# A first phase in another written order, with another share of VectorE's and GpSimd's work, and block 1's first product in another PSUM bank

## The chip, the cores and the metric

The kernel runs on one core of a Trainium2 chip. The metric is the time of one execution on the device, in microseconds (us). Before the change the median of three runs was 705.74 us (705.36 to 707.13).

The engines, as the profile names them: PE is TensorE (matmuls), PEld its weight loads, DVE is VectorE, ACT is ScalarE, POOL is GpSimd, SP is SyncE, which here only issues transfers. Each engine works through its own queue in the order in which the program was written.

## The reference

For each of 8 batches (8 heads, 576 rows, head width 64), 32 packed queries first attend over the rows, and the rows then attend over the 32 packed results. Then a gated feed-forward step with 2048 hidden columns runs on all 4608 rows.

```
s = q @ k.T / sqrt(64); s = s - max(s); a = exp(s); a = a / (sum(a) + 1e-9)   # sm_attn(q, k, v) = a @ v
p_packed = sm_attn(p, k, v)
out      = sm_attn(q, p_packed, p_packed)          # per batch and head
x = out, heads side by side: (4608, 512)
h = x @ w_in                                       # (4608, 2048)
g = h * clip(h + 3, 0, 6) / 6
result = g @ w_out                                 # (4608, 512)
```

The two weights come in as 64-bit floats; everything else is 32-bit.

## The kernel before

The hidden columns are cut into 16 blocks of 128, numbered f = 0 to 15. For a batch the kernel does not form x: it multiplies the packed results with `w_in` once (the matrix m), so that h is a product of the row weights a and m. Every factor of a large product is kept as two parts, `hi` (rounded) and `lo` (the rest), and a product is three matmuls: hi by hi, lo by hi, hi by lo.

The first batch runs in a first phase of its own, with the making of the weights and the attention of the second batch woven in; the other seven batches follow in a steady loop that the change does not touch. The order of the first phase stands in a table, `PLAN`: some 600 words, each the name of a chain. A chain is a generator (a list of steps); at each word the next step of that chain is written, and its instruction goes to the end of its engine's queue. So the table sets the order in all queues at once, SP's too. A second table, `ENGINES`, says on which engine a step runs where there is a choice (`on` and `copy`, lines 309 to 316).

The chains that matter here:

- `liF`, `loF` load block F of `w_in` and `w_out`; `in` was one chain for all inputs of the first batch, in a fixed order.
- `aF` (`w_in_step`) makes block F of `w_in` in 32 bits: two passes on ScalarE (L255, L257), a shift on VectorE (L261), an addition on GpSimd (L265). `bF` (`w_out_step`) does the same for `w_out`, then copies the hi part (L275) and subtracts for the lo part (L277).
- `m0`, `m1`, `m2`, `m4`, `m8`, `m12` (`u_m0`) multiply the packed results with blocks 0, 1, 2 to 3, 4 to 7, 8 to 11 and 12 to 15 of `w_in` (L336), and split the result (L347, L349). `m4` needs the additions of blocks 4 to 7, `m8` those of 8 to 11.
- `z0`, `z1` are the scores of rows against packed results; `z0a`, `z1a`, `z1b` turn them into a: maximum (L923), subtraction (L925), exponential, sum, division (L935), transposition (L937), hi (L939) and lo (L941).
- `hF` (`first`, L670) is the first product of block F, `rF` (`gates`) its gate: relu on ScalarE (L1333), minimum and product on VectorE (L1335), hi part `gh` (L1340), lo part `gl` (L1342). `yF` copies the gate's edge columns (L1349). `xF` is the second product (L1037), twelve matmuls into four accumulators.
- `S`, `E`, `V`, `T`, `Z`, `M` are parts of the second batch's attention.

All first products `hF` write the same PSUM tile pair `ps_h0`, of which there is one: `h1` has to wait until the gate of block 0 has read it. Where PE would have nothing to do, `keep_busy` (L202) multiplies zeros: in `warm` (1, 2 and 3 times), before `m1`, in `z1`, in `v1` and, six times, before `m2`. A matmul in 32 bits leaves two records in the trace.

Of the kernel before, what the change touches and what calls it, by code (L numbers as in the profile page):

```python
# [94 lines left out]
s0 warm q1 e0 q1 c0 c0 q0 e0 li0 b2 in v0 q0 e1 c1 v0 in v0 s1 s1 a0 qr c1 qr v0 z0 a0 z0 a0 z0a li2 z0a z0a e1
z0a in v1 a2 a2 a2 in v1 z0a z0a q2 li1 q3 q3 q2 z0a z0a z0a v1 a0 v1 z1 z1 a1 a2 m0 a1 a1 z0a z1b z0a a1 m0 z1a
li3 z1b a3 a3 upper z1a m0 z1b z1b a3 z1a lo0 m0 z1b z1a m0 m1 warm b0 z0a li4 z1a a4 a4 z1a lo1 z1b a3 b0 b0
z1b z1a m2 b1 z1b z1a z1b z1b b0 z1a z1a li7 z1a b1 z1b a7 a7 lp b1 h0 a7 h0 r0 b1 r0 li5 m1 m1 warm m1 h1 b0 m1
# [10 lines left out]
Z x11 lo13 b13 b13 b13 y10 r12 r12 r12 b13 Z b13 Z Z x11 r12 h13 h13 x12 x12 x12 r13 y12 r13 Z b13 lo14 h14 b15
Z y12 b15 r13 Z b14 b14 r13 b14 h14 Z b14 x13 r14 r14 x13 Z b14 x12 Z y13 b14 h15 Z x13 r14 h15 r15 x13 r14 x14  # L110
Z Z x14 y15 M r15 r15 Z y13 r15 x15 x15 x14 Z Z x14 o0 Z o0 x15 Z x15 Z Z o1 stage M M y15 y14 M M o2 o2 o3 o3
o1 y14
# [22 lines left out]
def packed_attention_moe(  # L135
# [542 lines left out]
    def first_attention(chains, homes):  # L678
# [33 lines left out]
        def inputs():  # L712

            t = wr.tile([P, 2, 2 * NB], F32, name="k_nat0", tag="w_in1")
            nat["k", 0] = long_rows(k, 0, 4, t[:, 0])
            yield
            nat["p"] = ap.tile([P, NG, D], F32, name="p_nat0", tag="pn", bufs=1)
            nc.scalar.dma_start(out=nat["p"], in_=p[0].rearrange("(g h) i d -> (h i) g d", g=NG))
            yield
            nat["k", 1] = long_rows(k, 4, 4, t[:, 1])  # L720
            yield
            nat["kr"] = rest_rows(nc.scalar, room(15, H * 2 * D), k)
            yield
            for g in range(NG):
# [820 lines left out]
```

## Time and profile before

| | us |
|---|---|
| median of three runs | 705.74 (705.36 to 707.13) |
| span of the profiled execution | 702.6 |
| first phase, to the first matmul of the steady loop | 116.74 |
| PE busy | 690.6 (98%) |
| DVE busy | 500.5 (71%) |
| ACT busy | 428.7 (61%) |
| POOL busy | 386.8 (55%) |

The page has the profiled execution's time only as its span, from the first to the last instruction; the 3.1 us to the runs' median lie around it. A row of the timeline gives the start in us from the span's start, the duration, the engine, the source line, the operation, what it writes and reads, the partitions and elements, and in brackets the idle time before it with what ended it. The duration of a VectorE record that stood blocked holds the time it was blocked.

### The profile page before, as it was taken

What the parts mean: (1) busy time and instruction counts of PE and PEld (TensorE: products, weight loads), DVE (VectorE), ACT (ScalarE), POOL (GpSimd) and SP (SyncE); (2) the same over time, 40 slices, a digit from 0 to 9 for tenths busy, and PEclk for the clock granted to TensorE, in tenths of its full rate; (3) what the DMA queues carried; (4) which work ended last, traced back from release to release, by engine and by line L of the source; (5) the groups of instructions that cost most, each with busy time, mean ns of one, the idle gap of its engine ahead of it and who ended that gap; (6) DMA issues with size and microseconds to landing.
All of it is one profiled execution on the core that took longest, in us unless ns stands there. A gap on an engine that the chain in (4) does not pass through costs nothing.

```text
span 702.6 us, 16232 instructions
## 1 busy us (share of the span) xinstructions
PE 690.6 (98%) x5944; PEld 595.8 (85%) x5944; DVE 500.5 (71%) x1087; ACT 428.7 (61%) x1014; POOL 386.8 (55%) x620
## 2 busy tenths in 40 slices
PE   7899999999999999999999999999999999999997
PEld 5587877888979888898898988899898988989997
DVE  4898788768899669774687667876488766864443
ACT  4898886556656656564465655666366665755453
POOL 1556662545645565575554555566455646657563
PEclk9999999999999999999999999999999999999999
DMA  9989852983429665655446755483543835341030
GB/s 270 318 208 259 227 130 83 285 176 120 100 105 242 139 168 186 158 147 126 126 150 158 157 134 181 130 211 70 129 166 128 198 85 182 120 140 41 32 105 31
DMA packets 199104, 107.50 MB, mean 153 GB/s; under 512 B 173424, under 2 KB 185200, under 8 KB 195440
## 3 DMA queue, kind: packets, MB, share of 16 engines
q1 hardware_dynamic: 198480, 106.26, 55.4%
q8 instruction: 47, 0.77, 0.5%
q14 instruction: 33, 0.27, 0.1%
q10 hardware_dynamic: 544, 0.20, 0.1%
HBM read 89.65 MB, written 16.78 MB: 151 GB/s over the span
## 4 chain that ended last, share of the span: by engine, by line
PE 87%; DVE 6%; DMA 2%; ACT 2%; issue 1%; POOL 1%; SPq 0%; DVEq 0%; ACTq 0%
PE acc L1037 49%; PE ps_hh L997 24%; PE ps L413 6%; PE ps_h L670 3%; PE ps L1037 2%; PE ps L533 1%; DMA v_nat<-in_v_dram 1%; DMA room<-in_q_dram 1%; PE ps L503 1%; ACT t L1333 0%; DVE osb L1236 0%; SPq L706 0%; DVE t L1335 0%; PE ps L336 0%; DVE t L1009 0%
## 5 line engine op out<-in xcount | busy, mean ns | idle before, releaser
L997 PE MATMUL ps_hh<-a_hi,m_hi 128*128 128x320 f32 (+1 forms) x448 | 133.8, 299 | 0.4 <-PE acc L1037 0.3
L997 PE MATMUL ps_hh<-a_lo,m_hi 128*128 128x320 f32 (+1 forms) x448 | 132.9, 297 | 0.0
L997 PE MATMUL ps_hh<-a_hi,m_lo 128*128 128x320 f32 (+1 forms) x448 | 132.8, 296 | 0.0
L1009 DVE SCALAR_TENSOR_TENSOR t<-t,ps_hh 128x320 f32<-128x320 f32 (+1 forms) x148 | 66.0, 446 | 78.3 <-ACT t L1008 73.4
L1037 PE MATMUL acc<-wo_hi,g 128*128 128x512 f32 x288 | 103.4, 401 | 0.0
L1008 ACT ACTIVATE t<-ps_hh,three 128x320 f32<-128x320 f32 (+1 forms) x148 | 73.7, 500 | 44.8 <-PE ps_hh L997 39.3
L1015 POOL TENSOR_TENSOR gf<-tb,gf 128x256 fp32r<-128x256 f32 x76 | 62.3, 821 | 64.6 <-ACT gf L1014 57.9
L997 PEld LDWEIGHTS ps_hh<-a_hi,m_hi 128*128 128x128 f32 x448 | 84.7, 189 | 9.2 <-DVE t L1009 2.8
L997 PEld LDWEIGHTS ps_hh<-a_lo,m_hi 128*128 128x128 f32 x448 | 84.7, 189 | 4.4 <-issue 1.4
L997 PEld LDWEIGHTS ps_hh<-a_hi,m_lo 128*128 128x128 f32 x448 | 84.7, 189 | 2.2 <-issue 1.7
L1015 POOL TENSOR_TENSOR g<-t,g 128x256 fp32r<-128x256 f32 x72 | 55.1, 768 | 39.1 <-ACT g L1014 36.3
L1037 PE MATMUL acc<-wt,ga 128*128 128x256 f32 x456 | 74.4, 283 | 0.0
L1037 PE MATMUL acc<-wo_hi,ge 128*128 128x256 f32 x304 | 71.5, 285 | 0.0
L1037 PEld LDWEIGHTS acc<-wo_hi,g 128*128 128x128 f32 x288 | 52.8, 189 | 13.5 <-ACT g L1014 2.1
L1037 PEld LDWEIGHTS acc<-wt,ga 128*128 128x128 f32 x456 | 63.4, 190 | 0.7 <-issue 0.5
L1015 POOL TENSOR_TENSOR ga<-t,ga 128x256 fp32r<-128x256 f32 x76 | 60.5, 795 | 2.0 <-ACT ga L1014 1.8
L1037 PEld LDWEIGHTS acc<-wo_hi,ge 128*128 128x128 f32 x304 | 53.1, 190 | 6.6 <-issue 2.3
L1037 PE MATMUL acc<-wo_lo,g 128*128 128x512 f32 x144 | 56.8, 395 | 0.0
L618 DVE STREAM_TRANSPOSE tr<-nat 128x576 f32<-128x576 f32 x56 | 42.6, 767 | 18.2 <-DMA nat<-in_q_dram 8.8
L1008 ACT ACTIVATE tb<-ps_hh,three 128x256 f32<-128x256 f32 (+1 forms) x76 | 37.9, 499 | 26.5 <-PE ps_hh L997 24.9
L1279 POOL TENSOR_TENSOR tb<-tb,t 128x128 f32<-128x128 f32 x76 | 38.5, 507 | 27.4 <-DVE t L1274 26.7
L1033 POOL COPY bnd<-t 128x64 f32<-128x64 f32 x76 | 21.6, 284 | 55.1 <-DVE t L1009 54.9
(227 smaller groups left out, 1845.9 us busy)
## 6 DMA issues: line engine op xcount, KB each, us to landing
w_again<-w_kept SPq DMA_DIRECT2D x24, 1024.0 KB, 4.8
wt<-t_kept SPq DMA_DIRECT2D x24, 768.0 KB, 5.1
out_dram<-osb SPq DMA_DIRECT2D x33, 256.0 KB, 2.4
nat<-in_k_dram SPq DMA_DIRECT2D x112, 72.0 KB, 3.1
nat<-in_q_dram SPq DMA_DIRECT2D x112, 72.0 KB, 3.0
raw_in<-in_moe_w_in_dram SPq DMA_DIRECT2D x10, 512.0 KB, 6.1
raw_out<-in_moe_w_out_dram SPq DMA_DIRECT2D x10, 512.0 KB, 4.1
w_kept<-w_in_sb SPq DMA_DIRECT2D x4, 1024.0 KB, 7.5
```

What stands on the lines that cost most here:

```text
L413: nc.tensor.matmul(pair[x][NPK * a:NPK * a + NPK, :n], rows[half, a], c, start=True, stop=True)
L503: nc.tensor.transpose(out=pair[x][:, c * P:(c + 1) * P], in_=e[x][:, c * P:(c + 1) * P], identity=ident)
L533: nc.tensor.matmul(pair[x][cols, :D], l, r, start=(c == 0), stop=(c == NST - 1))
L618: nc.vector.transpose(out=t, in_=state.pop(("nat", which, b, a)))
L670: nc.tensor.matmul(h[:, hf, :HS], mm[:, g, fs], aa[:, hf * HS:(hf + 1) * HS], start=(g == 0 and i == 0), stop=(g == NG - 1 and i == 2),)
L997: state["first"] = nc.tensor.matmul(h[:, :n], mm[:, g, fs], aa[:, t0:t0 + n], start=(g == 0 and i == 0), stop=(g == NG - 1 and i == 2),)
L1008: state["relu"] = nc.scalar.activation(out=t[:, :n], in_=h, func=AF.Relu, bias=three)
L1009: state["gate"] = nc.vector.scalar_tensor_tensor(out=t[:, :n], in0=t[:, :n], scalar=6.0, in1=h, op0=ALU.min, op1=ALU.mult)
L1015: engine.tensor_sub(out=lo, in0=x, in1=hi.bitcast(F32))
L1033: nc.gpsimd.tensor_copy(out=bnd[:, f, side * REM:side * REM + REM], in_=t[:, boff:boff + REM])
L1037: nc.tensor.matmul(out, lhs[x], rhs[y], start=first and i == 0, stop=last and i == 2, skip_group_check=True)
L1279: nc.gpsimd.tensor_sub(out=s4, in0=b1, in1=s2)
```

## The change

The order table is new up to the second batch's transpositions (`E`); from there on the words are the same. The chain `in` is cut into eleven chains that stand apart in the table (`ik0`, `ip`, ...), so that rows 512 to 575 of the queries and their second quarter are loaded ahead of the values, and block 0 of `w_out` is loaded ahead of blocks 1 and 3 of `w_in`. More steps have a choice of engine (the hi copies `whF`, `ghF`, `mhF`, `ah`, and the subtraction `zs`), and the table `ENGINES` gives some steps to another engine. `h1` writes the pair of banks in which the first scores stood (`homes["w"]`); the word `upper`, where that pair is given away, stands later for it, and `m2` takes its banks from the accumulators that are not in use yet. The six matmuls by zero before `m2` are gone, and one `warm`.

```diff
 PLAN = """
-in k0 in in p p k0 k1 k1 k2 k2 lo2 in kr b2 b2 b2 b2 kr k3 k3 in in in b2 s0 s0 s0 s0 s0 s0 s1 s1 s1 s1 s1 s1 s0
+ik0 k0 ip ik1 p p k0 k1 k1 k2 k2 lo2 ikr iqr iq1 kr b2 b2 b2 b2 s0 kr k3 k3 iv0 s0 s0 b2 s1 s0 iq0 s0 s0 q1 s1 s1
...
 ENGINES = {
-    "gl2": "D", "wl3": "D", "wl4": "D", "bl3": "P", "gl3": "D", "wl5": "D", "bl4": "D", "gl4": "D",
+    "D", "bl3": "P", "gl3": "P", "wl5": "P", "bl4": "D", "gl4": "D", "bl2": "D", "gl5": "D", "bl5":
...
     def w_out_step(f):
         yield from narrowed(f, "out")
         x = state.pop(("w", "out", f))
-        nc.scalar.copy(out=wo_at("hi", f), in_=x)
+        copy(f"wh{f}", wo_at("hi", f), x)
...
         for x, ps in enumerate(banks):
-            nc.scalar.copy(out=hi[:, x, to], in_=ps[:, :n * P])
+            copy(f"mh{fs[0]}{x}", hi[:, x, to], ps[:, :n * P])
...
+            for i in range(2):
+                chains[f"ik{i}"] = keys(i)
+                chains[f"iv{i}"] = values(i)
+            for a in range(NPAIR):
+                chains[f"iq{a}"] = queries(a)
+            chains["ip"], chains["ikr"], chains["iqr"] = packs(), key_rest(), query_rest()
...
-            nc.vector.tensor_sub(out=z[:, w], in0=z[:, w], in1=across(mx))
+            on(f"zs{g}{w.start}", "D").tensor_sub(out=z[:, w], in0=z[:, w], in1=across(mx))
...
-            nc.scalar.copy(out=hi[:, cols], in_=at[:, cols])
+            copy(f"ah{g}{w.start}", hi[:, cols], at[:, cols])
...
         def first(f):
-            h = tops[f] = ps_h0.tile([P, 2, 512], F32, name="ps_h0", tag="w")
+            h = tops[f] = (homes["w"] if f == 1 else ps_h0).tile([P, 2, 512], F32, name="ps_h0", tag="w")
...
-            nc.scalar.copy(out=hi, in_=top)
+            copy(f"gh{f}", hi, top)
...
             if f in (2, 4, 8, 12):
-                chains[f"m{f}"] = u_m0(list(range(f, 4 * (f // 4 + 1))), ahead=6 * (f == 2))
+                chains[f"m{f}"] = u_m0(list(range(f, 4 * (f // 4 + 1))), homes["tail"] if f == 2 else None)
```

What the tables move is seen in the queues. First GpSimd's, from the addition of block 1 of `w_in` to that of block 6 (x_out is a block of `w_out`, w_in_sb a block of `w_in`). Before:

```order
L265 TENSOR_TENSOR w_in_sb_322<-w_in_sb_322,raw_in 128x512
L941 TENSOR_TENSOR a_lo<-room,a_hi 128x576
L265 TENSOR_TENSOR w_in_sb_322<-w_in_sb_322,raw_429 128x512
L935 TENSOR_TENSOR z<-z,den_396 128x288
L265 TENSOR_TENSOR x_out<-x_out,raw_out 128x512 x2
L265 TENSOR_TENSOR w_in_sb_525<-w_in_sb_525,raw_in 128x512
L265 TENSOR_TENSOR x_out<-x_out,raw_429 128x512
L265 TENSOR_TENSOR w_in_sb_525<-w_in_sb_525,room 128x512
L265 TENSOR_TENSOR w_in_sb_525<-w_in_sb_525,raw_612 128x512
L265 TENSOR_TENSOR w_in_sb_525<-w_in_sb_525,room 128x512
```

And now, the same stretch of GpSimd's queue in the changed kernel:

```order
L270 TENSOR_TENSOR w_in_sb_325<-w_in_sb_325,raw_in 128x512
L946 TENSOR_TENSOR z<-z,mx_399 128x288
L962 TENSOR_TENSOR a_lo<-room,a_hi 128x576
L270 TENSOR_TENSOR w_in_sb_325<-w_in_sb_325,raw_415 128x512
L956 TENSOR_TENSOR z<-z,den_400 128x288
L270 TENSOR_TENSOR x_out<-x_out,raw_out 128x512
L962 TENSOR_TENSOR a_lo<-room,a_hi 128x288
L270 TENSOR_TENSOR x_out<-x_out,raw_out 128x512
L1363 TENSOR_TENSOR gl<-t,gh 128x512
L270 TENSOR_TENSOR w_in_sb_514<-w_in_sb_514,raw_in 128x512
L1370 COPY bnd<-t 128x2x32
L270 TENSOR_TENSOR x_out<-x_out,raw_415 128x512
```

GpSimd has taken over from VectorE the subtraction of half of `z1` (L946), half of the lo part of a (the second L962) and the lo part of block 0's gate (L1363).

Then TensorE's queue at the seam of block 0's and block 1's first product (ps_h is the pair of banks they write; L202 and L207 are the matmuls by zero). Before:

```order
L670 MATMUL ps_h_518<-a_hi,m_hi 128x288
L670 MATMUL ps_h_518<-a_lo,m_hi 128x288
L670 MATMUL ps_h_518<-a_hi,m_lo 128x288
L202 MATMUL ps_t<-pps 128x256 x3
L670 MATMUL ps_h_545<-a_hi,m_hi 128x288
L670 MATMUL ps_h_545<-a_lo,m_hi 128x288
```

And now:

```order
L675 MATMUL ps_h_471<-a_hi,m_hi 128x288
L675 MATMUL ps_h_471<-a_lo,m_hi 128x288
L675 MATMUL ps_h_471<-a_hi,m_lo 128x288
L675 MATMUL ps_h_537<-a_hi,m_hi 128x288
L675 MATMUL ps_h_537<-a_lo,m_hi 128x288
L675 MATMUL ps_h_537<-a_hi,m_lo 128x288
```

The matmuls by zero between the two blocks are gone, and block 1's tile (537) lies in another bank pair than block 0's (471).

Last SP's queue of transfers behind the last query loads (raw_in is block 1 of `w_in`, raw_429 and raw_415 block 3, raw_out block 0 of `w_out`). Before:

```order
L706 DMA room<-in_q_dram 128x2x256 x2
L238 DMA raw_in<-in_moe_w_in_dram 128x4x256
L238 DMA raw_429<-in_moe_w_in_dram 128x4x256
L238 DMA raw_out<-in_moe_w_out_dram 128x1024
L238 DMA room<-in_moe_w_in_dram 128x4x256
```

And now:

```order
L713 DMA room<-in_q_dram 128x2x256 x2
L243 DMA raw_out<-in_moe_w_out_dram 128x1024
L243 DMA raw_in<-in_moe_w_in_dram 128x4x256
L243 DMA raw_415<-in_moe_w_in_dram 128x4x256
L243 DMA room<-in_moe_w_in_dram 128x4x256
```

Block 1 of `w_in` is now second behind the queries, and block 3 third.

## Rows read from the trace of the kernel before

**Rows 1.** The page's top: span, and busy time of each engine

```profile
span 702.6 us, 16232 instructions
PE 690.6 (98%) x5944; PEld 595.8 (85%) x5944; DVE 500.5 (71%) x1087; ACT 428.7 (61%) x1014; POOL 386.8 (55%) x620
```

**Rows 2.** Busy by stretch: length, PE, PEld, DVE, ACT, POOL, clock, DMA, GB/s

```profile
24.50:46.04 21.54, 19.53 (x129) 15.82 (x130) 19.31 (x45) 19.63 (x40) 14.44 (x11) 1.00 0.91 244
46.04:65.65 19.61, 19.33 (x139) 14.89 (x138) 16.39 (x31) 17.07 (x32) 11.43 (x12) 1.00 0.95 244
65.65:91.90 26.25, 26.25 (x253) 20.82 (x252) 20.17 (x41) 22.78 (x42) 16.98 (x17) 1.00 0.91 241
```

**Rows 3.** TensorE's timeline, 33 to 67 us

```profile
33.55 1.46 PE L202 MATMUL ps_t<-pps 128*128 128x256 f32 x6
35.49 0.37 PE L670 MATMUL ps_h<-a_hi,m_hi 128*128 128x288 f32 x1 [0.48 <-ACT wo_hi L275]
...
37.15 0.40 PE L1037 MATMUL acc<-wo_hi,gh 128*128 128x512 f32 x1
...
46.63 1.09 PE L336 MATMUL ps<-w_in_sb,pp 64*32 64x512 f32 x16
...
53.26 0.72 PE L413 MATMUL ps_w<-tr,p_tr 64*32 64x288 f32 x16 [0.28 <-DVE t L1335]
...
66.48 1.09 PE L336 MATMUL ps<-w_in_sb,pp 64*32 64x512 f32 x16
```

**Rows 4.** VectorE's timeline, 35 to 44 us

```profile
35.66 1.13 DVE L277 TENSOR_TENSOR wo_lo<-x_out,wo_hi 128x512 fp32r<-128x512 f32 x1
36.71 0.68 DVE L1342 TENSOR_TENSOR gl<-t,gh 128x512 fp32r<-128x512 f32 x1
37.31 0.68 DVE L277 TENSOR_TENSOR wo_lo<-x_out,wo_hi 128x512 fp32r<-128x512 f32 x1
37.92 0.41 DVE L261 TENSOR_SCALAR x_out<-raw 128x512 int32<-128x512 int32 x1
38.25 0.74 DVE L1335 SCALAR_TENSOR_TENSOR t<-t,ps_h 128x576 f32<-128x576 f32 x1
...
43.22 0.94 DVE L261 TENSOR_SCALAR w_in_sb<-room 128x512 int32<-128x512 int32 x1
```

**Rows 5.** GpSimd's timeline, 24 to 85 us

```profile
24.50 1.29 POOL L265 TENSOR_TENSOR w_in_sb<-w_in_sb,raw_in 128x512 int32<-128x512 int32 x1 [2.10 <-ACT raw_in L257]
...
30.17 0.81 POOL L935 TENSOR_TENSOR z<-z,den 128x288 f32<-128x288 f32 x1 [0.77 <-DMA room<-in_moe_w_in_dram]
...
34.94 1.29 POOL L265 TENSOR_TENSOR w_in_sb<-w_in_sb,raw_in 128x512 int32<-128x512 int32 x1
...
42.55 1.32 POOL L265 TENSOR_TENSOR w_in_sb<-w_in_sb,raw 128x512 int32<-128x512 int32 x1
...
64.33 1.32 POOL L265 TENSOR_TENSOR w_in_sb<-w_in_sb,raw_in 128x512 int32<-128x512 int32 x1 [1.11 <-ACT raw_in L257]
...
83.16 1.30 POOL L1342 TENSOR_TENSOR gl<-t,gh 128x512 fp32r<-128x512 f32 x1 [0.24 <-ACT gh L1340]
```

**Rows 6.** Busy and count in 24.50 to 65.65: L265, L261, L277, L1342

```profile
24.50:65.65 41.15, 23.25 (x17) 1.00 0.93 244
24.50:65.65 41.15, 8.00 (x16) 1.00 0.93 244
24.50:65.65 41.15, 4.98 (x6) 0.00 (x0) 1.00 0.93 244
24.50:65.65 41.15, 4.16 (x6) 0.00 (x0) 1.00 0.93 244
```

**Rows 7.** SP's timeline: issue of the load of block 3 of `w_in`

```profile
14.12 2.54 SPq L238 DMA_DIRECT2D raw<-in_moe_w_in_dram  x1
```

**Rows 8.** Transfers issued at 14.12: count, KB each, us to landing

```profile
raw<-in_moe_w_in_dram SPq DMA_DIRECT2D x1, 512.0 KB, 9.7
```

**Rows 9.** ScalarE's timeline: first pass over block 1 of `w_in`

```profile
23.15 0.71 ACT L255 ACTIVATE raw_in<-raw_in 128x512 f32<-128x512 f32 x1
```

More of the change, by code (lines that the diff above doesn't have):

```diff
@@ L93 @@
 PLAN = """
-in k0 in in p p k0 k1 k1 k2 k2 lo2 in kr b2 b2 b2 b2 kr k3 k3 in in in b2 s0 s0 s0 s0 s0 s0 s1 s1 s1 s1 s1 s1 s0
[L95 to L98, printed above, removed]
@@ L109 @@
[L109 to L112, printed above, removed]
+ik0 k0 ip ik1 p p k0 k1 k1 k2 k2 lo2 ikr iqr iq1 kr b2 b2 b2 b2 s0 kr k3 k3 iv0 s0 s0 b2 s1 s0 iq0 s0 s0 q1 s1 s1
+li0 warm s1 s0 e0 q1 c0 c0 q0 s1 s1 s0 e0 v0 v0 q0 c1 qr v0 iv1 e1 v0 li2 iq2 z0 s1 iq3 qr s1 z0 a0 a0 c1 e1 a0
@@ new lines @@
+z0a z0a lo0 z0a v1 a2 a2 z0a z0a a2 q2 li1 v1 q3 q3 v1 q2 b2 a1 z0a a0 z0a z0a v1 z0a a1 z1 z1 a2 z0a a1 z0a li3
+m0 z1a m0 z1b a3 z1a z1b z1a a3 a1 warm z1a z1b z1b m0 li4 m1 a3 z1b lo1 m1 z1a z1b z0a b0 z1a m0 z1a a3 b0 h0
+li5 m2 a4 b1 b0 z1a z1b z1b b0 b1 m0 z1b a4 z1a z1a m2 z1b z1a m1 li7 m2 m1 m1 a7 a7 a7 lp a4 z1b lo3 lo5 h0 li6
+r0 b1 h1 b0 r0 m2 h1 h2 b0 b1 m2 r0 r0 h2 r1 b1 x0 r1 x0 x0 b3 r1 a7 b3 b1 b3 y0 r1 b5 y0 y1 x1 x1 x0 y1 upper a6
+lo4 lo6 r2 h3 a5 b3 r2 x1 a5 a5 lk0 b4 a6 x1 a4 tk0 r2 a6 b4 r2 b4 b3 a5 x2 b5 y2 h3 lk2 a6 r3 b4 m4 x2 tk2 b3 x2
@@ new lines @@
+tp lk3 b5 r3 m4 r3 m4 h4 m4 li8 y3 tk3 b4 m4 lk1 h4 r3 x3 b6 b4 x3 tk1 b6 b6 r4 below y3 li9 a8 b5 a8 lo8 x2 S b6
+y4 b5 r4 y4 S S b5 a9 a8 li10 x3 S a8 S a9 x3 h5 r4 h5 a10 r4 x4 y2 b6 lq1 r5 x4 a9 r5 a9 b6 y5 a10 r5 S S b8 x4
+a10 a10 h6 r5 li11 b8 S x4 h6 b8 x5 r6 a11 a11 x5 x5 b8 b8 y5 S r6 x5 a11 a11 h7 h7 b8 m8 lo9 tq1 lq3 b9 S r6 r6
+lo7 b7 lo10 x6 b7 x6 li13 b7 tq3 lq2 x6 r7 y7 r7 b9 x6 m8 r7 m8 b7 m8 li12 h8 b10 m8 lq0 b7 h8 y7 b7 r7 x7 x7 b10
+y6 y6 x7 a13 r8 lo12 b10 r8 a13 b9 tq2 r8 b10 S S b10 lv r8 h9 h9 y8 r9 S S b10 x8 a13 x8 r9 tq0 a12 x7 y9 x8 h10
@@ new lines @@
+h10 a12 b9 S b9 E r9 S b12 E b12 r10 y10 E y8 lw1 y9 x8 r9 E a13 b9 x9 x9 S h11 a12 r10 a12 E E b12 r10 r10 lo11
+b11 h11 E b11 b11 r11 x10 r11 lw0 b11 li14 a14 V a14 V V a14 li15 x10 T b12 x9 T x9 a14 Z a15 a15 x10 a15 x10 Z Z
+r11 Z y11 lo15 Z b11 a15 b12 b15 m12 r11 b15 b11 m12 b15 b15 y11 x11 m12 m12 m12 b12 x11 h12 h12 Z x11 lo13 b13
+b13 b13 y10 r12 r12 r12 b13 Z b13 Z Z x11 r12 h13 h13 x12 x12 x12 r13 y12 r13 Z b13 lo14 h14 b15 Z y12 b15 r13 Z
+b14 b14 r13 b14 h14 Z b14 x13 r14 r14 x13 Z b14 x12 Z y13 b14 h15 Z x13 r14 h15 r15 x13 r14 x14 Z Z x14 y15 M r15
@@ L113 @@
+r15 Z y13 r15 x15 x15 x14 Z Z x14 o0 Z o0 x15 Z x15 Z Z o1 stage M M y15 y14 M M o2 o2 o3 o3 o1 y14
 """
 ENGINES = {
[10 rows of a table removed]
[16 rows of a table added]
 }
@@ L689, in tail @@
             return ps_o.tile([P, 512], F32, name="ps_t", tag=f"acc{(tails[0] - 1) % 4}", bufs=1)
+        homes["tail"] = tail
         def wide(i):
@@ L712, in inputs, with keys, packs, key_rest @@
         def inputs():
[L714 to L724, printed above, removed]
+            kt_ = wr.tile([P, 2, 2 * NB], F32, name="k_nat0", tag="w_in1")
+            def keys(i):
+                nat["k", i] = long_rows(k, 4 * i, 4, kt_[:, i])
+                yield
+            def packs():
+                nat["p"] = ap.tile([P, NG, D], F32, name="p_nat0", tag="pn", bufs=1)
+                nc.scalar.dma_start(out=nat["p"], in_=p[0].rearrange("(g h) i d -> (h i) g d", g=NG))
+                yield
+            def key_rest():
+                nat["kr"] = rest_rows(nc.scalar, room(15, H * 2 * D), k)
+                yield
+            def values(g):
                 t = wp.tile([P, 4 * NST * D], F32, name="v_nat0", tag="v_nat", bufs=1) if g == 0 else room(12, 4 * NST * D)
@@ L728, in inputs, with queries, query_rest @@
                 yield
-                for a in (2 * g, 2 * g + 1):
-                    nat["q", a] = long_rows(q, 2 * a, 2, room(4 + a, 8 * D))
-                    yield
-                if g == 0:
-                    nat["qr"] = rest_rows(nc.sync, room(10, H * 2 * D), q)
-                    yield
+            def queries(a):
+                nat["q", a] = long_rows(q, 2 * a, 2, room(4 + a, 8 * D))
+                yield
+            def query_rest():
+                nat["qr"] = rest_rows(nc.sync, room(10, H * 2 * D), q)
+                yield
+            for i in range(2):
[4 more added lines that the diff above has]
+            chains["ip"], chains["ikr"], chains["iqr"] = packs(), key_rest(), query_rest()
         def turn_rows(x, i, place):
@@ L955, in warm @@
                 yield
-        chains["in"] = inputs()
+        inputs()
         chains["warm"] = warm()
```

10 lines of the change are left out of this document (removed), and 24 rows, old and new, of the table ENGINES.

## The prediction

> **What bounds the kernel now.** I read the page's top first: PE is busy 98% of the span, and no other engine more than 71% [rows 1]. That says the steady loop runs at PE's pace, and the change does not touch that loop. So I read the first phase alone, by stretches. From 24.50 to 65.65 us PE is busy nearly throughout, but VectorE is at 90% and 84% of the two stretches, ScalarE at 91% and 87%, and GpSimd at 67% and 58% [rows 2]. A busy share of 67% looks like room. The next view, the timelines of VectorE and GpSimd side by side, shows that it is not.
>
> A lo part on VectorE (L277) and a lo part of the gate (L1342) take 0.68 us alone. The L277 at 35.66 took 1.13: GpSimd was in an addition from 34.94 to 36.23, and VectorE's operation ended at 36.79, so it began at about 36.11 (36.79 less 0.68). The shift L261 takes 0.41 alone; the one at 43.22 took 0.94, and GpSimd's addition beside it ran from 42.55 to 43.87 [rows 4, 5]. So these VectorE operations and GpSimd's do not run side by side: they take turns. I call the two together the pair: all that GpSimd does, the shift L261, and VectorE's operations on two tensors of SBUF. L277 is one of these; that L1342, L925, L935 and L941 take turns too I assume from their being of the same kind.
>
> How full is the pair? From the addition of block 1 of `w_in` (24.50) to that of block 11 (64.33, over at 65.65) are 41.15 us. In them stand 17 additions on GpSimd, 16 shifts, and 6 and 6 lo parts on VectorE [rows 6], and besides one a_lo of 576 columns, one division and three small copies on GpSimd, and five operations of 288 columns on VectorE. I price them by what one keeps the pair: an addition 1.29, the division 0.81 [rows 5]; a shift 0.33 (37.92 to 38.25) and a lo part 0.60 (36.71 to 37.31) [rows 4]. By columns, as estimates from these: a_lo 1.45 (1.29 x 576/512), a VectorE operation of 288 columns 0.34. The small copies are on both sides and are taken at 0.25, an estimate from the 1.29 for 512 columns. The sum is 17 x 1.29 + 1.45 + 0.81 + 0.75 + 16 x 0.33 + 12 x 0.60 + 5 x 0.34 = 39.1. Only 2.05 of 41.15 us are free. To this comes what overlaps when one engine hands over: above, VectorE began 0.12 before GpSimd's record ended. With about 20 such turns that is up to 2.4 more. Free in all: 2 to 4.4 us.
>
> PE meanwhile runs `m4` at 46.63 and `m8` at 66.48 [rows 3], 0.83 after the last addition that `m8` needs. So PE and the pair are both full, and whichever the change makes longer sets the end.
>
> **The change, part by part.** *Block 1's banks and the matmuls by zero.* Before, the six records of zeros at 33.55 and a wait of 0.48 fill the time until `h1` starts at 35.49 [rows 3]: 1.94 us, in which the gate of block 0 frees the banks. In other banks `h1` follows block 0's last matmul at once, so PE gains 1.94 there. The zeros ahead of `m2` also go; they stood in the wait for the second half of `z1`, which stays, so I cost them at nothing.
>
> Here the clock may answer. The granted clock is 1.00 in every stretch of [rows 2], with those zeros in place. [...] It is the third rival.
>
> *The loads.* Block 1 of `w_in` now stands second behind the queries; that place belonged to block 3, which was issued at 14.12 and landed 9.7 later, at 23.8 [rows 7, 8]. Everything ahead of it in the queue is the same set of loads in another order, so I take 23.8 as its landing. Before, ScalarE began on block 1 at 23.15 and GpSimd added at 24.50 [rows 5, 9], 1.35 later. Now ScalarE begins at about 23.8 and GpSimd at about 25.05 to 25.15, some 0.55 later. If the queries' new place brings the loads forward, the bound is zero.
>
> *The tables of engines.* To the addition of block 11 GpSimd gets four lo parts more (`gl0`, `gl3`, `wl5`, `wl6`) and two half operations (a subtraction of `z1`, half of a_lo). On GpSimd a lo part takes 1.30 (L1342 at 83.16) and a half operation 0.81 [rows 5]: 4 x 1.30 + 2 x 0.81 = 6.8. VectorE gives up 4 x 0.60 + 2 x 0.34 = 3.1. It gets two copies from SBUF to SBUF (`gh4`, `wh6`), of which this trace has no row: between the shift's 0.33, the same columns with one input, and the lo part's 0.60; I take 0.33, nearest by kind, so 0.7. [...] The stem of the matter: an operation moved off VectorE leaves 0.60 behind and asks 1.30 of the pair. The pair gets 6.8 - 3.1 + 0.7 = 4.4 us longer. VectorE itself gets 2.4 us shorter; that would count if VectorE alone, not the pair, set the pace.
>
> *What is late next.* GpSimd's queue is strict: the additions of blocks 8 to 11 stand behind the new lo parts. Before, the last ended at 65.65. Now it ends at 65.65 + 0.55 + 4.4 less what of the free 2 to 4.4 us gets filled: 70.6 at most, 66.2 at least. The queues are full and one engine mostly waits for the other, so part of the free time will be used: I take half of the 4.4, giving 68.4. PE, which gains 1.94 at `h1`, would reach `m8` at 64.5, waits at `m4` and `m8`, and starts `m8` at about 68.4 instead of 66.48: 1.9 us late. Behind `m8` PE is busy 26.25 of 26.25 us [rows 2] with the same work, so it cannot catch up, and the phase ends 1.9 later.
>
> **Sum.** Against the profiled span of 702.6 [rows 1]: 702.6 + 1.9 = 704.5. The runs' median of 705.74 is 3.1 above the span; I take that as unchanged: 707.6. With the pair's bounds, -0.2 to +4.1, this case alone lies between 705.5 and 709.8. A measurement of this kernel can tell about 0.3%, 2.1 us, from no change: faster is under 703.6, slower over 707.9. So the forecast itself lies just inside "no change", and its upper part outside.
>
> **The rivals.** *PE sets the pace (faster).* For it: PE is busy 19.53 of 21.54 and 19.33 of 19.61 us, VectorE loses 2.4 us of work, and the order could place the pair's turns without a gap. Then the 1.94 at `h1` stays, and with it the 0.28 wait at 53.26 [rows 3] goes: 705.74 - 2.2 = 703.5. Against it: the pair's sum, which would need more than all its free time.
>
> *The gain is given back (no change).* PE comes 1.9 earlier to `m4`, waits there, and the pair fills all of its 4.4 free us, so that `m8` starts where it did. 705.7. For it: the free time is just as long as what is added. Against it: the later start of block 1, and that no queue is without a gap.
>
> [...]
>
> **How the numbers follow.** Forecast 0.50, PE's pace 0.20, given back 0.17, clock 0.13. Slower by over 0.3%: the clock's 0.12 and about half of the forecast, 0.24, in all 0.36. Faster: 0.16 of PE's pace and a little beside it, 0.17. The rest, 0.47, is within 0.3%. The range takes in the first two rivals nearly whole and the upper bound of the pair: 703.5 to 710.0.
>
> **What would show it.** Right: `m4` and `m8` begin behind a wait for GpSimd (L270, additions of `w_in`), `m8` at 67.5 or later; GpSimd's and VectorE's records stretch each other more than before; `h1` follows block 0 without a gap; block 1's addition starts after 24.8. Wrong: `m8` before 66 with no wait ahead of it; block 1's addition before 24.5; or a stretch with a granted clock under 1.00, which would make the third rival the cause. If the steady loop, from its first matmul on, is not as long as before, something lies outside of all this.

## The result and the profile after

The changed kernel takes 710.76 us (median of 6, 709.84 to 712.08) against 706.36 for the kernel before on the same chip: a ratio of 1.006, with a 95% interval of 1.0042 to 1.0078, so 3.0 to 5.5 us longer. A second set gave 710.77 and 1.0064 (1.0043 to 1.0085). Two executions of one experiment below (the kernel before with cut additions), which took 950.77 and 1111.33 us at a granted clock of 0.66 and 0.56, are left out of its numbers. The forecast was 707.6, with 710.0 as the upper end: too low, and the likeliest case, "no change", did not come.

The top of the page of the changed kernel, to be held against [rows 1]:

```profile
span 709.9 us, 16191 instructions
PE 693.3 (98%) x5926; PEld 595.6 (84%) x5926; DVE 505.8 (71%) x1089; ACT 425.4 (60%) x1005; POOL 398.0 (56%) x627
```

The span grew by 7.3 us, the median by only 4.4. Both spans are single executions; a profiled execution's own time is its span and 1.8 (709.9 and 711.72 here). By that the profile of before was of a quick execution, some 704.4, and not of the median: of the 3.1 us that were said to lie around its span, only 1.8 do. For this reason I reckon from here on from `m0`, the first use of the finished weights: in a second profile of the kernel before (an experiment below) `m4`, `m8` and `m12` come within 0.05 us of where they came in the first, reckoned from `m0`.

The stretches `m0` to `m4`, to `m8`, to `m12`, first of the kernel before, then of the changed kernel (columns as in [rows 2]):

```profile
23.83:46.63 22.80, 20.79 (x172) 16.46 (x156) 20.50 (x47) 20.81 (x43) 14.45 (x11) 1.00 0.90 241
46.63:66.48 19.85, 19.57 (x142) 15.37 (x141) 16.47 (x31) 17.31 (x33) 12.25 (x12) 1.00 0.98 256
66.48:92.08 25.60, 25.60 (x248) 20.15 (x247) 19.68 (x41) 22.13 (x40) 16.15 (x15) 1.00 0.90 235
```

```profile
23.32:48.41 25.09, 20.32 (x154) 16.16 (x138) 22.28 (x44) 20.53 (x40) 18.20 (x15) 0.80 0.77 216
48.41:70.58 22.17, 20.56 (x143) 15.29 (x142) 20.24 (x31) 16.19 (x30) 15.60 (x13) 1.00 0.85 217
70.58:99.70 29.12, 26.65 (x246) 19.93 (x246) 22.73 (x47) 21.18 (x38) 17.85 (x15) 1.00 0.84 218
```

Each stretch is longer: by 2.29, 2.32 and 3.52 us. In all three VectorE and GpSimd are busier, and in the first the granted clock is 0.80 on average. From the first matmul of the steady loop (124.11) to the end the time is as before, 585.8.

The clock by pieces of 2 us:

```profile
28.00:30.00 2.00, 0.93 (x5) 0.70 (x5) 1.97 (x5) 2.00 (x4) 1.66 (x2) 0.86 1.11 320
30.00:32.00 2.00, 0.58 (x16) 0.26 (x16) 1.97 (x6) 0.79 (x2) 1.92 (x2) 0.50 1.03 371
...
36.00:38.00 2.00, 2.00 (x10) 2.00 (x10) 1.55 (x3) 1.81 (x4) 1.25 (x2) 0.50 0.92 146
38.00:40.00 2.00, 2.00 (x12) 2.00 (x11) 0.82 (x3) 1.45 (x3) 2.00 (x2) 0.58 0.48 69
```

TensorE had been busy 0.93 and then 0.58 of 2 us when the granted clock went to 0.50. TensorE's timeline, to be held against [rows 3]:

```profile
31.42 1.11 PE L341 MATMUL ps_t<-w_in_sb,pp 64*32 64x256 f32 x16 [2.04 <-DVE m_lo L354]
...
34.07 0.61 PE L675 MATMUL ps_h<-a_lo,m_hi 128*128 128x288 f32 x1 [0.92 <-DVE a_lo L962]
...
35.43 0.44 PE L675 MATMUL ps_h<-a_hi,m_hi 128*128 128x288 f32 x1
...
40.52 0.40 PE L1058 MATMUL acc<-wo_hi,gh 128*128 128x512 f32 x1
...
48.41 1.09 PE L341 MATMUL ps<-w_in_sb,pp 64*32 64x512 f32 x16
51.99 0.37 PE L675 MATMUL ps_h<-a_hi,m_hi 128*128 128x288 f32 x1 [0.90 <-DVE t L1356]
...
70.58 1.09 PE L341 MATMUL ps<-w_in_sb,pp 64*32 64x512 f32 x16 [0.28 <-POOL w_in_sb L270]
...
91.90 0.32 PE L538 MATMUL ps<-v_high,et 128*32 128x64 f32 x8 [1.17 <-DMA v_high<-in_v_dram]
...
99.70 1.09 PE L341 MATMUL ps<-w_in_sb,pp 64*32 64x512 f32 x16 [0.52 <-POOL w_in_sb L270]
```

`h1` does follow `h0` without a gap (35.43), but at a granted clock of 0.50 its matmuls start 0.24 apart instead of 0.13. `m2` waits 2.04 for its banks, which `m_lo` of `m1` reads. `x0` starts 17.20 after `m0` instead of 13.32; 1.6 of that is `h2`, which now stands ahead of it. The other 2.3 are all of the 2.29 by which `m4` is late: from `x0` to `m4` TensorE takes 7.89, and before 9.48 with `h2`. Behind `m4`, `h4` waits for `t`, the gate of an earlier block, on VectorE. What VectorE and GpSimd do ahead of that wait:

```profile
41.94 1.31 DVE L1370 COPY bnd<-t 128x64 f32<-128x64 f32 x1
...
45.38 1.13 DVE L266 TENSOR_SCALAR w_in_sb<-raw 128x512 int32<-128x512 int32 x1
...
47.03 1.54 DVE L266 TENSOR_SCALAR x_out<-room 128x512 int32<-128x512 int32 x1
...
49.19 1.47 DVE L282 TENSOR_TENSOR wo_lo<-x_out,wo_hi 128x512 fp32r<-128x512 f32 x1
...
51.11 0.74 DVE L1356 SCALAR_TENSOR_TENSOR t<-t,ps_h 128x576 f32<-128x576 f32 x1
```

```profile
41.65 1.54 POOL L270 TENSOR_TENSOR x_out<-x_out,raw 128x512 int32<-128x512 int32 x1 [0.51 <-ACT raw L262]
...
44.90 1.33 POOL L270 TENSOR_TENSOR w_in_sb<-w_in_sb,room 128x512 int32<-128x512 int32 x1 [0.42 <-DVE w_in_sb L266]
46.64 1.64 POOL L270 TENSOR_TENSOR w_in_sb<-w_in_sb,raw 128x512 int32<-128x512 int32 x1 [0.42 <-ACT room L262]
48.80 1.30 POOL L270 TENSOR_TENSOR x_out<-x_out,room 128x512 int32<-128x512 int32 x1 [0.52 <-DVE x_out L266]
```

Each of the first four VectorE records begins while an addition runs, and ends shortly after it: the shift at 47.03 ends at 48.57 (47.03 and 1.54), the addition beside it at 48.28 (46.64 and 1.64). The four end 0.06, 0.28, 0.29 and 0.56 after their additions, each 0.12 to 0.13 less than the same operation takes alone (0.19, 0.41, 0.41, 0.68). So nearly the whole operation stands behind the addition: 1.54 for a shift that takes 0.41 alone [rows 4], 1.31 for a copy of 64 columns that takes 0.19 elsewhere. VectorE is never idle from 40 to 52. I added this up from `m0` to `m12`: for each kind of VectorE operation the duration that a fifth of its records do not exceed counts as undisturbed, and what single records are over that by more than 0.15 us as held up. Before, 5.9 of 56.65 busy us are held up; after, 14.6 of 65.25. What is left is about the same, 50.7. The sums depend on which operations are taken as one kind (with another grouping they move by up to 2 us, here to 5.0 and 15.1), so only large differences between them count.

### The profile page after: what moved, and what is told of

Same layout as the page of the kernel before. It is cut to its first block, busy times and chain, and to the rows that moved or that the text cites. A ratio compares the mean times of both kernels' runs of the same rounds, so it can differ in the third digit from the quotient of the medians.

```text
span 709.9 us, 16191 instructions
## 1 busy us (share of the span) xinstructions
PE 693.3 (98%) x5926; PEld 595.6 (84%) x5926; DVE 505.8 (71%) x1089; ACT 425.4 (60%) x1005; POOL 398.0 (56%) x627
## 4 chain that ended last, share of the span: by engine, by line
PE 86%; DVE 6%; DMA 3%; issue 2%; SPq 1%; ACT 1%; POOL 1%; ACTq 0%; DVEq 0%; POOLq 0%
PE acc L1058 49%; PE ps_hh L1018 25%; PE ps L418 6%; PE ps_h L675 2%; PE ps L1058 2%; DMA room<-in_q_dram 1%; PE ps L538 1%; DMA raw_in<-in_moe_w_in_dram 1%; DMA room<-in_k_dram 1%; PE ps L508 1%; DVE x_out L266 1%; DVE t L1356 1%; DVE gl L1363 0%; DVE wo_lo L282 0%; DVE w_in_sb L266 0%
## 5 line engine op out<-in xcount | busy, mean ns | idle before, releaser
L1029 ACT ACTIVATE tb<-ps_hh,three 128x256 f32<-128x256 f32 (+1 forms) x76 | 38.0, 500 | 25.8 <-PE ps_hh L1018 23.8
```

The costliest lines, as they stand in the source:

```text
L1029: state["relu"] = nc.scalar.activation(out=t[:, :n], in_=h, func=AF.Relu, bias=three)
```

## The experiments

Theories. C: the fallen clock is the cause. P: the table gives GpSimd more work, and the pair gets longer. O: the written order puts VectorE's operations beside GpSimd's additions, so that VectorE is held up whatever the sum of work. L: the loads. Later runs part O further, under names that their expectations explain. Each run is held against the kernel before in its own set (705.5 to 707.1).

### Clock: zeros put back in the changed kernel, too many and then sized

```diff
 for g in range(NG):
+    if f == 0 and g == 0:
+        keep_busy(h[:, 0], 4)     # sized: 2
+    if f == 0 and g == 1:
+        add_zeros(h[:, 0], 8)     # sized: 4; adds zeros to h0's own bank
     gemm1(h, f, g)
+    if f == 0 and g == 0:
+        add_zeros(h[:, 0], 9)     # sized: 4
```

> The changed kernel with 21 matmuls by zero put back on TensorE, where it stood idle: 4 ahead of block 0's first product, 9 behind that product's first half (ahead of m2), 8 ahead of its second half; the last two groups add zeros to block 0's own bank and so wait for no bank. Theory C (the clock: TensorE had too little to do from 26 to 35 us, fell to half clock, and all that came later follows from the late gate of block 1): granted clock 1.00 from 28 to 40 us, the 12 matmuls of block 1 in about 1.7 us instead of 2.9, x0 at 38.3 to 39 instead of 40.5, m4 at about 46.6, the waits for the values of the second batch (91.9) gone or small, time 706 to 708. Theory P (VectorE and GpSimd in turns set the pace, the clock is hidden behind them): granted clock 1.00 as well, but m4 at 48 or later and h4 at about 51.5 behind a wait, time within 1 us of the changed kernel's 710.8.

712.64 (1.0061 to 1.0103 of before). The zeros took twice the room I had meant (two records each) and pushed `m2` to 33.63. Sized:

> The changed kernel with matmuls by zero sized to the gaps: 2 ahead of block 0's first product, 4 behind its first half, 4 ahead of its second half (each is two passes of 0.23 us, so the 21 of the first trial took 9.8 us and pushed m2 from 31.4 to 33.6 and block 1's product behind). Theory C (the clock alone): clock 1.00 throughout, m2 at about 31.4 as in the changed kernel, x0 at about 39 instead of 40.5, m4 at 46.7 to 47.5, time 707 to 709. Theory O (the new written order places VectorE's operations where GpSimd's hold them up; VectorE is then the limit): m4 within 0.5 us of 48.4 reckoned from m0, h4 behind a wait for VectorE as before, time within 1 us of 710.8.

710.02 (1.0045 to 1.0089). The stretches 28 to 38 of the sized run:

```profile
28.00:30.00 2.00, 1.74 (x11) 1.37 (x10) 1.97 (x5) 2.00 (x6) 1.87 (x2) 1.00 1.12 318
30.00:38.00 8.00, 7.65 (x59) 6.32 (x58) 6.52 (x19) 6.03 (x13) 4.95 (x5) 1.00 1.12 316
```

The clock stays at 1.00, `m4` comes 24.26 after `m0` instead of 25.09 (before: 22.80), and `h4` waits 0.93 for `t` as it did. `x0` is on time again, 14.82 after `m0` with `h2` ahead of it, but then TensorE waits for VectorE's lo parts of the gates, for which it did not wait in the changed kernel:

```profile
41.49 0.50 PE L1063 MATMUL acc<-wo_hi,gl 128*128 128x512 f32 x1 [0.46 <-DVE gl L1374]
...
46.56 0.50 PE L1063 MATMUL acc<-wo_hi,gl 128*128 128x512 f32 x1 [0.28 <-DVE gl L1374]
```

What the clock gives back, 0.8 us, shows in the trace at `m4`; in the time the intervals of the changed kernel with and without the fall lie on each other. So C falls as the cause of the loss.

### Clock: the kernel before without those zeros

```diff
-    ... u_m0(list(range(f, 4 * (f // 4 + 1))), ahead=6 * (f == 2))
+    ... u_m0(list(range(f, 4 * (f // 4 + 1))), ahead=0)
-li5 m1 m1 warm m1 h1
+li5 m1 m1 m1 h1
```

> The kernel before without the 6 matmuls by zero ahead of m2 (27.65 to 30.34 with their kind) and without the third group of three ahead of block 1's product; nothing else changes. Theory C: the granted clock falls to 0.50 for some us between 28 and 38, block 1's 12 matmuls are 0.24 apart instead of 0.133, and the time rises by 2 to 4 us to 708.5 to 710.5. Theory P: whether the clock falls or not, the time stays within 1 us of 706.4, because m4 waits for the additions anyway.

708.82, 1.0027 (1.0007 to 1.0047): 0.5 to 3.3 us. The clock is at 0.50 from 32 to 40, and TensorE waits more:

```profile
31.05 1.11 PE L336 MATMUL ps<-w_in_sb,pp 64*32 64x256 f32 x16 [1.64 <-POOL w_in_sb L265]
...
37.63 0.58 PE L670 MATMUL ps_h<-a_hi,m_hi 128*128 128x288 f32 x1 [1.71 <-ACT wo_hi L275]
```

In the old order, where TensorE sets the pace, the zeros are worth some 2 us; in the new order nothing that can be measured.

### Table: six operations back to VectorE; four moved in the kernel before; the whole table

```diff
-"gl0": "P", "gl3": "P", "wl5": "P", "wl6": "P", "zs19": "P", "al19": "P", "gh4": "D", "wh6": "D"
+"gl0": "D", "gl3": "D", "wl5": "D", "wl6": "D", "zs19": "D", "al19": "D", "gh4": "A", "wh6": "A"
```

> The changed kernel with six operations moved back from GpSimd to VectorE (the lo parts gl0, gl3, wl5, wl6, the subtraction of z1's half and the lo part of that half) and two copies (gh4, wh6) back from VectorE to ScalarE; order, loads, banks and zeros stay as changed. Theory P: the pair's work shrinks by 4.4 us, m4 starts at 46 to 47.5, m8 at 67 to 68.5, the time falls by 2 to 4 us to 707 to 709. Theory C: the granted clock still falls to 0.50 from about 29 to 39 us, and the time stays within 1 us of 710.8.

711.39 (1.0048 to 1.0087): no gain. The clock fell as in the changed kernel (0.990 on average over the profiled run, there 0.992), GpSimd has 44.63 us of work from `m0` to `m12` instead of 51.65, VectorE is still held up for 12.9, and `m8` comes 47.33 after `m0` (47.26 in the changed kernel). P falls for the new order.

```diff
-"gl0": "D", "gl3": "D", "wl5": "D", "wl6": "D"
+"gl0": "P", "gl3": "P", "wl5": "P", "wl6": "P"      # in the kernel before
```

> The kernel before with four lo parts (gl0, gl3, wl5, wl6) on GpSimd instead of VectorE, nothing else. Each takes 0.68 on VectorE and 1.30 on GpSimd. Theory P: the pair gets 2.8 us longer (4 x 0.70) and GpSimd 5.2 us; with 2 to 4.4 us free in the pair the additions that m4 and m8 need come 1 to 3 us later, time 707.5 to 709.5. Theory C: the granted clock stays 1.00 and the time within 1 us of 706.4.

709.52 (1.0024 to 1.0052). The time is as P has it; the place is not: `m8` comes only 0.62 later (43.27), `m12` 1.13, and VectorE is held up 9.0. The whole table apart from the order:

```diff
 # changed kernel, table replaced          # kernel before, table replaced,
-ENGINES = {... the new table ...}         # with copy()/on() at wh, mh, ah, gh, zs
+ENGINES = {... the old table ...}
```

> The changed order, loads, banks and zeros with the whole table of engines of the kernel before. Theory P (the table makes the loss): time back to 706 to 708. Theory O (the order makes it): time 709.5 to 713, with VectorE's operations held up by at least twice the 5.8 us that they are held up in the kernel before from m0 to m12.

> The kernel before with the whole new table of engines (and the copies that it names on other engines); order, loads, banks and zeros as before. Theory P: 709 to 712, the whole of the loss. Theory O: 706.5 to 709, the part that the lo parts on GpSimd alone made (709.5 with four of them), and no fall of the clock.

New order with the old table: 711.25 (1.0059 to 1.0102). Old order with the new table: 709.89 (1.0042 to 1.0097). Each costs as much alone as both together; VectorE is held up 12.1 and 12.3 us. The first came as O has it, the second as P has it: in the old order the new table has a price of its own. But being held up is not yet being late: in the second run `m8` comes only 0.80 later than before (43.45) and `m12` 2.81, in the first 4.5 (47.14) and 5.4.

### The loads alone; the kernel before again

> The kernel before with only its loads in the changed order (and, since every queue but the loads' keeps its order, the same work on every engine). Theory L (the loads: v before q, lo0 ahead of li1 and li3, five loads ahead of the second batch's keys): m0 to m4 1 us or more longer, time 708 or more. Else (loads are worth nothing, as the prediction took it but for 0.55 us): m0 to m4 within 0.6 us of 22.8 and the time within 1 us of before.

The loads' words alone were moved in the kernel before. 706.83, 1.0006 (0.9984 to 1.0028); `m4` 22.62 after `m0`, `m8` 42.45, held up 5.6. L falls.

> The kernel before once more, unchanged, for a second profile. Its first profile shows a span of 702.6 against a median of 706 to 707 of the timed runs, while the changed kernel's 709.9 stands 0.9 under its median. If the first profile was of a quick execution, this span lies at 704 to 707, and the difference lies ahead of m0 (the landing of the first loads, m0 at 24.5 to 26 instead of 23.8). If the span is a fixed 3 us under the time, it is again 702 to 703.

Span 703.3; `m4`, `m8` and `m12` 22.76, 42.61 and 68.20 after `m0` (22.80, 42.65, 68.25 in the first profile). The spread lies ahead of `m0` (behind it both profiles take 678.8), as expected of a quick first profile, though the span itself was below the 704 to 707 named.

### New order to x0 and old behind it; old order to x0 and new behind it

Both with the old table; the words of one plan up to the first `x0`, then the remaining words in the order of the other.

> The changed order, loads, banks and missing zeros up to block 0's second product (x0), from there the old order; the whole table of the kernel before. It stands between the kernel before and the changed order with the old table (711.25 in the last set, 5.7 over before). Theory O1 (the loss lies in the stretch up to x0: fall of the clock, later weights): m4 about 25 us after m0 as there, from m4 to m8 some 20 to 22, time 709 to 711. Theory O2 (the loss lies in the stretch from x0 to m8, where VectorE is held up): m8 at most 44 us after m0 and the time 706 to 708.

> The old order, zeros and banks up to x0, from there the changed order; the whole table of the kernel before. Theory O1: m0 to m8 in at most 43.5 us (42.65 before), time 706 to 707.5. Theory O2: clock 1.00, m4 to m8 takes 21 to 22.5 us instead of 19.85, the time 708.5 to 711.

710.07 (1.003 to 1.0059) and 710.92 (1.0035 to 1.0076). In the first `m4` is late (25.75) and the stretch to `m8` takes 20.44, so most of its loss up to `m8` lies ahead of `m4`. The second is no clean half: without banks of its own for block 1, `h2`, now ahead of `x0`, waits 1.84 for the gate of block 1; the granted clock is 0.998 on average over the profiled run. So the first half alone costs about half of what the whole order does with the old table (0.44 of 0.81%); what the second costs by itself is not shown.

### Block 1's banks alone, in the kernel before

Besides the lines below, the word `upper` stands later, two groups of zeros are gone and the copies of `m2` stand ahead of `x0`.

```diff
-h = tops[f] = ps_h0.tile(...)
+h = tops[f] = (homes["w"] if f == 1 else ps_h0).tile(...)
-chains[f"m{f}"] = u_m0([f], tail, f)
+chains[f"m{f}"] = u_m0([f], tail, 2 * f)
-... u_m0(..., ahead=6 * (f == 2))
+... u_m0(..., homes["tail"] if f == 2 else None, ahead=8 * (f == 2))
```

> The kernel before with only block 1's product in the banks of the first scores; m2 in banks of the tail, 8 matmuls by zero ahead of m2 and 2 ahead of m1 in place of 6, 1 and two groups between, so that the clock stays up; loads and table as before, m2's last three copies ahead of x0. If TensorE's pace bounds this stretch: block 1's product follows block 0's without the 1.94 us of zeros and waiting, x0 some 1.5 us earlier, time 704 to 705.5 (before 705.5 to 706.5). If the additions for m4 bound it (prediction's step): x0 earlier but m4 again 22.8 us after m0, time within 0.7 us of before. If the clock falls: 707 or more.

708.81 (1.0012 to 1.0043). `h1` now waits for ScalarE's copy of `m1`:

```profile
37.00 0.40 PE L670 MATMUL ps_h<-a_hi,m_hi 128*128 128x288 f32 x1 [1.04 <-ACT m_hi L347]
```

Behind that wait the clock falls as well (0.50 from 38 to 40), so this is the case that the expectation puts at 707 or more. With that copy moved ahead, and `h2` ahead of `x0`:

> The kernel before with block 1's product in the banks of the first scores, as in the earlier trial of that part alone, but m1's four copies ahead of block 0's gate (ScalarE's copy for m1 held block 1's product up by 1.04 there) and block 2's product ahead of x0, which cannot start before the lo part of gate 0 at 37.4. Prediction's step (the additions on GpSimd bound m4, 2 to 4.4 us of free time): TensorE reaches x1 1 to 1.9 us earlier, m4 comes 22 to 22.8 us after m0 and the time is within 0.7 us of before. If TensorE's pace bounds: m4 21 us after m0, time 1.5 to 2 us less than before. If it is slower by over 1 us, the copies and the bank have a price of their own.

710.85 (1.004 to 1.0087). Now `h2` waits for the copy of `m2`:

```profile
40.39 0.40 PE L670 MATMUL ps_h<-a_hi,m_hi 128*128 128x288 f32 x1 [2.59 <-ACT m_hi L347]
```

From `m0` to `m12` the granted clock is 0.98 on average (26.09 to 98.46). Both trials failed to show the gain: the banks only let `h1` go early if the copies that read them, on ScalarE, go early too. Whether the pair had free time for such a gain stays open.

### Additions cut, in both orders

```diff
-nc.gpsimd.tensor_tensor(out=xi, in0=xi, in1=low, op=ALU.add)
+nc.gpsimd.tensor_tensor(out=xi[:, :64], in0=xi[:, :64], in1=low[:, :64], op=ALU.add)
```

> The changed kernel with the sized zeros, and every addition of w_in and w_out on GpSimd cut from 512 to 64 columns; the other 448 columns keep the shifted high word, so the low words are missing there. The order, and which operation waits for which, stay the same. Theory T (the new order places VectorE's operations beside GpSimd's, which hold them up: 15 us from m0 to m12 against 5.9 before): GpSimd is busy a third as long, VectorE is held up for at most 5 us, the waits of TensorE at h4, m8 and m12 go, and the time comes down by 4 us or more, to 704 to 706, level with the cut kernel before or under it. Theory Q (order and queues in themselves, whatever GpSimd's operations take: VectorE's work stands in another sequence): the time comes down by under 2 us, to 708 or more, and stays 3 us or more over the cut kernel before.

> The kernel before with the same cut of the additions to 64 columns (the low words of 448 columns are missing). It is the measure for the cut changed kernel. TensorE is already busy 98% here and waits little from m0 to the steady loop (some 2 us), so both theories expect 704 to 706.5, at most 2 us under the kernel before.

> The same without the cut: changed order, sized zeros, the whole table of the kernel before. With the clock falling it was 711.25, 5.7 over before. Clock 1.00 from 28 to 40 us. Theory T: the pair's work is that of the kernel before, but VectorE is still held up for about 12 us; time 708.5 to 710.5, so 2 to 4 over its cut twin. If the clock was the larger part of the 5.7: 707 to 708.5, within 1 of the cut twin.

> The changed order with the sized zeros, the whole table of the kernel before, and the additions cut to 64 columns (the low words of 448 columns are missing). The same cut with the new table came to 707.8, 2.1 over the cut kernel before. Theory T (turn-taking is the cause and the order in itself is harmless): 705 to 707. Theory Q (a part of some 2 us is the order's own, whoever does the lo parts): 707 to 709.

| | time | over before, % (95%) | held up, `m0` to `m12` |
|---|---|---|---|
| before | 706.2 to 707.1 | 0 | 5.9 |
| before, cut | 705.38 | -0.07 (-0.27 to 0.14) | 0.5 |
| new order and table, zeros | 710.02 | 0.67 (0.45 to 0.89) | 15.3 |
| the same, cut | 707.79 | 0.19 (0.06 to 0.33) | 3.4 |
| new order, old table, zeros | 713.71 | 0.94 (0.77 to 1.10) | 12.1 |
| the same, cut | 708.87 | 0.27 (0.13 to 0.42) | 0.2 |

The stretch `m0` to `m12` whole, one fence for each: before; new order with the old table and zeros; its cut twin.

```profile
23.83:92.08 68.25, 65.96 (x559) 51.99 (x543) 56.65 (x117) 60.25 (x114) 42.85 (x37) 1.00 0.92 243
```

```profile
24.28:98.72 74.44, 68.77 (x561) 52.30 (x545) 62.71 (x118) 60.28 (x113) 42.84 (x37) 1.00 0.84 218
```

```profile
24.50:95.68 71.18, 68.18 (x561) 53.38 (x545) 50.29 (x115) 59.18 (x112) 16.16 (x37) 0.98 0.91 227
```

The second fence is the decisive row. GpSimd has 42.84 us of work against 42.85 before, ScalarE 60.28 against 60.25, and the clock is at 1.00: the same work. VectorE is busy 6.1 us longer, about what it is held up more (12.1 less 5.9), and the stretch is 6.2 longer. That the last two agree is no rule (the old order with the new table was held up as much and was 2.8 late). Cut the additions, and VectorE's 62.71 fall to 50.29, with 4.8 us of the time; the kernel before loses 26 us of GpSimd's work (42.85 to 16.90) to the same cut and gains nothing that can be measured. So in the new order O holds for most of the loss (4.8 of the 6.6 us over before): the price of an addition depends on what the order puts beside it.

The cut shortens GpSimd's own chain too, and no run parts the two. The waits speak for VectorE: in the run with sized zeros and the new table TensorE waits 2.9 us for VectorE from `m0` to `m12` and 1.6 for GpSimd; in that of the second fence 4.9 and 0.5, ScalarE waits for GpSimd once (0.7), and VectorE never waits for a result of GpSimd's. Its largest waits of TensorE, and the one for GpSimd (us in total, times, longest):

```profile
PE ps_t L340 <- DVE m_lo L353: 1.8, 1, 1.8
PE ps_h L674 <- DVE t L1361: 1.7, 2, 0.9
...
PE ps_t L340 <- POOL w_in_sb L269: 0.5, 1, 0.5
```

Not all of it is O. By the ranges set ahead, the cut kernel with the old table (708.87) falls to Q, which leaves some 2 us to the order itself, and that with the new table (707.79) lies between T and Q. The uncut kernel with the old table (713.71) came out above both of its ranges.

What is left under the cut, 0.19 and 0.27%, has a place in the trace. VectorE, then TensorE at `S`, of the cut kernel with the new table:

```profile
51.50 0.67 DVE L287 TENSOR_TENSOR wo_lo<-x_out,wo_hi 128x512 fp32r<-128x512 f32 x1
54.28 0.78 DVE L628 STREAM_TRANSPOSE tr<-nat 128x576 f32<-128x576 f32 x1 [2.10 <-DMA nat<-in_k_dram]
...
55.28 0.74 DVE L1367 SCALAR_TENSOR_TENSOR t<-t,ps_h 128x576 f32<-128x576 f32 x1
```

```profile
56.08 0.72 PE L423 MATMUL ps_w<-tr,p_tr 64*32 64x288 f32 x16 [1.60 <-DVE t L1367]
```

The keys of the second batch are late; in the other cut kernel VectorE waits 1.81 there and TensorE 1.91, and the clock is 0.93 on average from `m4` to `m8`. In the changed kernel itself VectorE never gets far enough ahead to wait for them. That this is all of the rest was not tried.

### The changed kernel again

> The changed kernel once more, on the same chip as the cut kernels, for its time beside theirs and a second profile. If its later stages are as regular as those of the kernel before (m0 to m8 42.65 and 42.61 in two profiles), then m4 again comes 25.0 to 25.2 us after m0, m8 47.1 to 47.4 and m12 75.5 to 76.5; if the wait for the values (1.17 at 91.90) was chance, m12 comes at 73.5 to 74.5 after m0 without it. The clock falls again to 0.50 between 29 and 40 us. Time 709.5 to 711.5.

710.77. `m4`, `m8` and `m12` come 25.06, 47.28 and 74.00 after `m0`, and the values are not waited for: the 1.17 at 91.90 was chance, and with it 2.4 of the 8.1 us by which `m12` came late in the first profile. Behind `m0` this profile takes 684.6 (the first 686.6, the kernel before 678.8). That is 5.8 more than before, against 4.4 between the medians, so the changed kernel must usually be quicker ahead of `m0`; no run shows that by itself. No run that computes all of the reference was faster than the kernel before.

## Why the prediction was wrong

- **Block 1's banks, +1.94 for TensorE.** That `h1` follows at once was right, that TensorE gains by it was wrong. `m2` waits 2.04 for its new banks and `h0` for a_lo, so TensorE reaches `x0` 17.20 after `m0`, 2.3 later than before when `h2` (1.6) is taken off. Even at a clock of 1.00 it is 14.82, or 13.2 without `h2`, level with the 13.32 before.
- **The zeros at nothing.** Wrong in the old order (0.5 to 3.3 us); in the new order they indeed bring nothing, but for another reason: VectorE comes last there.
- **The clock as third rival.** It fell to 0.50 where TensorE had little to do (busy 0.93 and 0.58 of 2 us from 28 to 32); with the sized zeros (1.74 of 2 us from 28 to 30) it stayed at 1.00. No row of before shows it under 1.00, so the chance of 0.13 was the author's estimate; what the runs show in its place is 0.8 us at `m4` and nothing measurable in the time of the new order. The prediction said that a fall would make this rival the cause. The sized zeros show that it did not: the clock at 1.00, and still 0.67% over before.
- **The loads, +0.55.** Too large: ScalarE had block 1 at 22.99 instead of the 23.8 forecast (23.15 before), and the loads alone cost nothing. The addition of block 1 began at 24.61 instead of 24.50 [rows 5], which is 0.6 late reckoned from `m0`, but it waited for VectorE's shift and not for the load.

```profile
22.99 0.77 ACT L260 ACTIVATE raw_in<-raw_in 128x512 f32<-128x512 f32 x1 [0.93 <-DMA raw_in<-in_moe_w_in_dram]
```

```profile
24.61 1.29 POOL L270 TENSOR_TENSOR w_in_sb<-w_in_sb,raw_in 128x512 int32<-128x512 int32 x1 [3.10 <-DVE w_in_sb L266]
```

- **The pair, +4.4, of which half would be hidden.** This is the step that failed: "part of the free time will be used: I take half of the 4.4", and with it `m8` 1.9 late. Reckoned from `m0`, `m8` is 4.6 late. That looks as if only the share hidden was mis-sized; but the sum itself does not decide. With the sum of the kernel before in the new order `m8` is 4.5 late (47.14), and 5.4 (48.00) with the clock held at 1.00; with four more lo parts on GpSimd in the old order it is 0.6 late, with the whole new table 0.8. The prediction priced the banks, the loads and the table and gave the new written order no term of its own; alone it costs 0.8 to 0.9%. What decides there is which VectorE operation stands beside an addition. Nor was the pair the limit before: with 26 us less of GpSimd's work the kernel before keeps its `m4` and `m8` (22.78 and 42.61). [Rows 2] had hinted at it, with PE busy 19.33 of 19.61 us in the second stretch; I took the pair for as full. Of the signs named, `m8` after 67.5 behind a wait for GpSimd came true (0.28); `m4` began without a wait.
- **Which operations take turns.** I counted those on two tensors of SBUF, the shift and, at 0.33, the copies. That a copy takes turns stood in none of the rows, so the 0.7 for `gh4` and `wh6` was the author's estimate. A copy of 64 columns was held 1.1 us too (1.31 instead of 0.19), and the copy of `gh` at 59.43, beside an addition from 59.22 to 60.52, took 1.38 instead of the 0.42 of a copy of the same size (`wo_hi`) in the same trace; the rows stand below. It began 0.21 after the addition and ended 0.29 after its end, so 1.09 of its 1.38 lie beside it. So a price per piece of work was the wrong unit: a short operation pays for what is left of the long one beside it, here 1.09 us.

```profile
59.22 1.30 POOL L270 TENSOR_TENSOR w_in_sb<-w_in_sb,raw_in 128x512 int32<-128x512 int32 x1 [0.36 <-DVE w_in_sb L266]
```

```profile
59.43 1.38 DVE L316 CAST gh<-t 128x512 fp32r<-128x512 f32 x1
...
61.55 0.42 DVE L316 CAST wo_hi<-x_out 128x512 fp32r<-128x512 f32 x1
```

- **Behind `m8`: it cannot catch up, and stays 1.9 late.** It did not stay: 4.6 at `m8`, 5.8 at `m12` in the second profile (8.1 in the first). The words behind `m8` are nearly the same, but VectorE and GpSimd keep their late turns there (22.73 and 17.85 us busy, 19.68 and 16.15 before), and TensorE waits at `m12`.
- **The base.** 702.6 was a quick execution. The forecast took the 3.1 between span and median as fixed, so it put its 1.9 on the median, which is right for a forecast of a median; but terms read from one quick trace hid the spread ahead of `m0`.
